# Sequence transform: right-hand sums as additions, and those of two products made by an adding DMA

## The chip, the cores and the metric

The kernel runs on one core of a Trainium2 chip. The metric is device time in microseconds (us), the median of several runs of the same program. A core has TensorE (PE, matrix products), VectorE (DVE), ScalarE (ACT), GpSimd (POOL) and SyncE (SP), each with its own queue of instructions that it works through in order; 16 DMA engines move blocks between HBM and the on-chip memory, and POOL, SP and ACT issue DMAs.

## The reference

The inputs are float32: x of 2048 x 1024, two 2048 x 2048 matrices of a sequence transform, two 1024 x 1024 matrices of a hidden transform, weights of a dense layer with 3584 hidden units, and a gate vector.

```python
g = sigmoid((x * gate_w).sum(-1, keepdims=True))
a = x @ Wd_re.T ;  b = x @ Wd_im.T              # hidden transform
y = Ws_re @ a - Ws_im @ b                       # sequence transform, real part
h = relu(x @ w1 + b1) ** 2 ;  o = h @ w2 + b2   # dense layer
return g * y + (1 - g) * o
```

## The kernel before, in words

There are four matrix stages, one after the other: X (the hidden transform, giving blocks `ab`), C (the sequence transform, giving `y`), H (first dense product) and O (second dense product). Between stages the blocks are kept in HBM tensors (`Kept`): `ab`, `h`, and `gy`, which is y times the gate.

Each stage cuts its product 2 x 2 and forms it from seven products instead of eight (Winograd's form), with sums S1 to S4 of left blocks and T1 to T4 of right blocks (L34 to L39). Within some products (`TWICE_C`) the same scheme is applied once more to part of the depth. Sign conventions: in C, the left blocks are `ab` and the right blocks are tiles of the input `ct`, the transposed transform matrices.

```python
TALL_C = (1, 2, 5, 6, 3, 7, 4)                    # order of the seven products (L19)
FACTORS = {... 5: ("S1", "T1"), 6: ("S2", "T2"), 7: ("S3", "T3")}
```

A block is 128 partitions x 1024 floats, 512 KB. Each operand block is split into a part `hi`, rounded by ScalarE (L221), and a rest `lo` = block - hi, made by VectorE (L231). A block product is then three matmuls per 128 x 128 tile: hi.hi, hi.lo, lo.hi (L307). Products 5, 6 and 7 of C go directly: 8 depth blocks x 2 column halves, 16 steps of 24 matmuls each. Per step there is one right sum, and per two steps one left sum.

A sum of two blocks that lie in HBM is a `Part` (L132). `load_parts` takes a buffer for each, and issues both loads on SP (L153). `make_parts` then has VectorE add or subtract them in place (L173), and frees the second buffer. T1 and T3 of product 5 and 7 are such sums of two `ct` blocks; T2 and T4 build on sums that are already on the chip, or on copies of them that POOL stores to HBM (`copy<-raw`) and SP fetches again.

The order of instructions is written out by a planner, the loop from L926. At step i of 434 it: issues loads up to 12 steps ahead (`LOADS`), as long as buffers are free and no more than `RAWS` = 4 blocks are loaded but not summed; issues the stores of results on POOL; makes sums and `hi` copies that are due within 3 steps (`SUMS`), or earlier if its own clock of VectorE says there is time; makes the `lo` rests due within 2 steps; then issues the step's matmuls. This fixes the order on each engine's queue. On the chip an engine goes ahead as far as its inputs and buffers allow, so SP, VectorE and ScalarE run some time ahead of TensorE.

When a product ends, its PSUM banks are copied to a buffer by ScalarE (`put`, L434), added to a buffer by VectorE (`add`, L440), or finished by `final` (L806 in C: y times the gate row, then a store to `gy` on POOL). The next product that builds on a buffer has ScalarE write it back into PSUM first (L294). The gate rows are fetched by `Row`; for O they are turned into 1 - g (L784).

Of the kernel before, what the change touches and what calls it, by code (L numbers as in the profile page):

```python
# [11 lines left out]
AF = mybir.ActivationFunctionType  # L12
# [30 lines left out]
def gated_mix_kernel(ctx: ExitStack, tc: tile.TileContext, x4, xn, w4, ct, w1a, w1b, w2, b1, b2, gw, out):  # L43
# [11 lines left out]
    nc = tc.nc  # L55
# [76 lines left out]
    class Part(Near):  # L132


        def __init__(self, a, b=None, op=None, width=512):
            super().__init__("part")
            self.blocks, self.op, self.width, self.copy = ([a] if b is None else [a, b]), op, width, None
            self.cuts = [(slice(0, 2), slice(0, width))]
            for e in self.blocks:
                if isinstance(e, (Near, View)):  # L140
                    e.uses += 1

        def room(self):
            return sum(not isinstance(b, (Near, View)) for b in self.blocks)

        def load_parts(self, engines):
            self.slots = [None if isinstance(b, (Near, View)) else take("raw") for b in self.blocks]
# [6 lines left out]
                yield  # L154

        def load(self, engines):
            run(self.load_parts(engines))

        def extra(self):
            return 0 if self.room() else 1  # L160

        def time(self):
            return VEC[0] + VEC[1] * self.width / 512 if self.op else 0.0

        def make_parts(self):
            for b in self.blocks:
                assert not isinstance(b, (Near, View)) or b.done
            src = [b.slot if isinstance(b, (Near, View)) else t for b, t in zip(self.blocks, self.slots)]
            mine = [t for t in self.slots if t is not None]
            self.slot, self.done = mine[0] if mine else take("sum"), True  # L170
            for k, c in self.cuts:
                if self.op:
                    nc.vector.tensor_tensor(self.slot[:, k, c], src[0][:, k, c], src[1][:, k, c], op=self.op)  # L173
# [153 lines left out]
            needs += group.done[count[group] // group.k - 1][1]  # L327
        wanted.append(needs)

    stores = []  # L330
    later, now = deque(), [0]
    clock = {"pe": 10.0, "vec": 0.0, "dma": 0.0}

# [3 lines left out]
    class Sums:  # L337


        def __init__(self, get, sums, keep=False, far=()):  # L340

            self.get, self.sums, self.keep, self.far, self.made = get, sums, keep, far, {}

        def of(self, key, width=512, near=False):
            if key in self.made:
                return self.made[key]
            if key not in self.sums:
                if not self.keep:
                    return self.get(*key)
                b = self.get(*key)  # L350
                e = b if isinstance(b, (Near, View)) else Part(b, width=width)
            else:
                a, b, op = self.sums[key]
                e = Part(*(self.of(p, width).far() if p in self.far and not near else self.of(p, width) for p in (a, b)), op, width)
            self.made[key] = e
            return e

# [52 lines left out]
                    ends[e] = len(steps)  # L410
        return ends

    def tall(left, right, ksteps, order, second, first, target, final, last=None):

# [1 line left out]

        left = {q: Sums(lambda i, j, q=q: left_(i, j, q), SUMS_L, far=FAR_TALL) for left_ in (left,) for q in range(ksteps)}
        right = {(q, c): Sums(lambda j, n, q=q, c=c: right_(j, n, q, c), SUMS_R, far=FAR_TALL) for right_ in (right,)
                 for q in range(ksteps) for c in range(2)}
        keys = [(c, rp) for c in range(2) for rp in range(2)]
# [12 lines left out]
        def add(dst, k, ps, ends=False, src=None, sign=1):  # L437
# [323 lines left out]
    class Row(Near):  # L761
# [1 line left out]

        ready = False

        def __init__(self, n, less):
            super().__init__("g")
            self.n, self.less, self.uses = n, less, 8

        def extra(self):  # L770
            return 0
# [7 lines left out]

        def sum(self):  # L780
            self.done = True
            if not self.less:
                return 0.0
            nc.vector.tensor_scalar(flat(self.slot), flat(self.slot), -1.0, 1.0, op0=ALU.mult, op1=ALU.add)  # L784
            return VEC[0] + VEC[1]

        def rest(self):
# [7 lines left out]
          for rp in range(2)}  # L795

    def c_stage():
        rows = [Row(n, False) for n in range(2)]
        to = {}

        def target(i, n, k):
            near = Near("y")
            to[near] = i, n, *k
            return near

        def final(dst, ps):  # L806
            i, n, c, rp = to[dst]
            nc.vector.tensor_tensor(dst.slot, dst.slot if ps is None else ps, rows[n].of(c).broadcast_to([P, 2, 512]),
                                    op=ALU.mult)
# [5 lines left out]
        tall(lambda i, j, q: ab[j, q, i], lambda j, n, q, c: ct[n, c, j, q], 8, TALL_C, TWICE_C, FIRST_C, target, final)  # L815
        return at, rows


    def o_stage():
        rows = [Row(n, True) for n in range(2)]  # L820
# [98 lines left out]
        o.landed = 0.0  # L919

    def ready(o):
        near = [o.block] if isinstance(o, Operand) else getattr(o, "blocks", ())
        return all(b.done for b in near if isinstance(b, (Near, View)))

    loaded = summed = rested = 4
    for i in range(-SUMS, n + LATER + 2):  # L926
# [5 lines left out]
        while loaded < len(items) and items[loaded].need <= i + LOADS:  # L932
# [11 lines left out]
            o.landed = clock["dma"] + LAND - RATE if o.room() else 0.0  # L944
            loaded += 1
        for dst, src, k, tiles in stores:
            if isinstance(dst, Kept):
# [73 lines left out]
```

## Time and profile before

| | us |
|---|---|
| three runs | 1882.75, 1888.65, 3587.61 |
| median | 1888.65 |
| span of the profiled execution | 1879.6 |
| TensorE matmul busy | 1866.2 |
| VectorE busy | 1686.0 |
| ScalarE busy | 1044.1 |
| GpSimd busy | 87.6 |

The span is the time from the first to the last instruction of one profiled execution; the time of a run also holds what lies around it, so the close runs lie 3.2 and 9.1 us above the span. The third run has almost twice the time of the others and is not used. A row of a group of instructions reads: line, engine, operation, what it writes and reads with shapes, count, busy time in all, mean ns of one, and the idle time just before them with what ended it. "L173" is line 173 of the kernel.

### The profile page before, as it was taken

The numbers are of one execution on the slowest core, as the hardware profiler recorded it, in microseconds if no ns is written. First come the engines' busy times: TensorE is split into PE (matmuls) and PEld (weight loads), VectorE is DVE, ScalarE is ACT, GpSimd is POOL, SyncE is SP. The second block draws the span as 40 slices with busy tenths as digits, with TensorE's granted clock in tenths as the row PEclk, the third lists the DMA queues.
The fourth block names the chain that finished last, engine by engine and source line by source line (L and its number), as shares of the span: only waits on it lengthen the run. The fifth ranks groups of instructions, "written<-read, shape, count | busy, mean of one in ns | idle before, by whom it ended". The sixth has DMA issues, their size and how long they took to land.

```text
span 1879.6 us, 22035 instructions
## 1 busy us (share of the span) xinstructions
PE 1866.2 (99%) x8228; PEld 1541.3 (82%) x8228; DVE 1686.0 (90%) x1638; ACT 1044.1 (56%) x1184; POOL 87.6 (5%) x162
## 2 busy tenths in 40 slices
PE   9999999999999999999999999999999999999998
PEld 7888888888888878888888888888888888887887
DVE  8997898599779898799996998799999998699898
ACT  6474563363343554366485797676977534264453
POOL 0000110000000000000000010000100000000000
PEclk9999999999999999999999999999999999999999
DMA  6732989439788379464461766536865798638971
GB/s 224 249 121 74 351 286 412 141 112 361 275 307 330 128 299 378 149 232 181 137 221 61 302 234 218 195 122 246 298 233 177 254 389 317 258 124 335 409 256 52
DMA packets 128570, 443.97 MB, mean 236 GB/s; under 512 B 14144, under 2 KB 23632, under 8 KB 128464
## 3 DMA queue, kind: packets, MB, share of 16 engines
q1 hardware_dynamic: 106560, 364.05, 53.7%
q0 software_dynamic: 21616, 78.14, 10.4%
q8 instruction: 64, 1.05, 0.2%
q10 hardware_dynamic: 288, 0.39, 0.1%
q14 instruction: 42, 0.34, 0.1%
HBM read 363.87 MB, written 78.65 MB: 235 GB/s over the span
## 4 chain that ended last, share of the span: by engine, by line
PE 94%; DVE 4%; DMA 1%; ACT 1%; issue 0%; SPq 0%; DVEq 0%; ACTq 0%
PE ps L307 94%; DVE lo L231 1%; DVE h L620 1%; DVE sum L173 1%; DMA raw<-in_x 0%; DVE u L503 0%; DMA raw<-in_w1b 0%; DMA g<-g_far 0%; DVE both L231 0%; DVE raw L173 0%; ACT ps L294 0%; ACT h L717 0%; ACT hi L221 0%; DVE o L505 0%; SPq L153 0%
## 5 line engine op out<-in xcount | busy, mean ns | idle before, releaser
L307 PE MATMUL ps<-hi 128*128 128x512 f32 x2168 | 844.3, 390 | 3.3 <-ACT hi L221 2.7
L307 PE MATMUL ps<-lo,hi 128*128 128x512 f32 x2168 | 844.1, 390 | 0.0
L307 PE MATMUL ps<-hi,lo 128*128 128x512 f32 x2168 | 843.3, 390 | 0.7 <-DVE lo L231 0.6
L221 ACT ACTIVATE hi<-raw 128x1024 fp32r<-128x1024 f32 (+2 forms) x398 | 406.8, 1037 | 370.6 <-DVE raw L173 245.7
L231 DVE TENSOR_TENSOR lo<-raw,hi 128x1024 fp32r<-128x1024 f32 (+2 forms) x398 | 468.3, 1197 | 45.5 <-ACT hi L221 28.4
L307 PEld LDWEIGHTS ps<-hi 128*128 128x128 f32 x2168 | 407.5, 188 | 89.7 <-ACT hi L221 3.5
L307 PEld LDWEIGHTS ps<-hi,lo 128*128 128x128 f32 x2168 | 407.6, 188 | 86.3 <-DVE lo L231 2.1
L307 PEld LDWEIGHTS ps<-lo,hi 128*128 128x128 f32 x2168 | 407.4, 188 | 84.4 <-DVE lo L231 0.4
L173 DVE TENSOR_TENSOR raw<-raw 128x1024 f32<-128x1024 f32 (+1 forms) x276 | 325.6, 1206 | 57.4 <-DMA raw<-in_ct 13.6
L307 PE MATMUL ps<-hi,both 128*128 128x512 f32 x1120 | 347.9, 390 | 3.1 <-ACT ps L294 3.1
L221 ACT ACTIVATE hi<-sum 128x1024 fp32r<-128x1024 f32 (+1 forms) x192 | 196.8, 1038 | 184.5 <-DVE sum L173 170.1
L231 DVE TENSOR_TENSOR lo<-sum,hi 128x1024 fp32r<-128x1024 f32 (+1 forms) x192 | 228.0, 1200 | 31.5 <-PE ps L307 18.2
L307 PEld LDWEIGHTS ps<-hi,both 128*128 128x128 f32 x1120 | 210.3, 188 | 49.4 <-ACT ps L294 5.5
L307 PE MATMUL ps<-lo,both 128*128 128x512 f32 x560 | 218.3, 390 | 0.1
L173 DVE TENSOR_TENSOR sum<-raw 128x1024 f32<-128x1024 f32 (+2 forms) x136 | 140.3, 1048 | 13.0 <-PE ps L307 9.3
L173 DVE TENSOR_TENSOR sum<-raw,sum 128x1024 f32<-128x1024 f32 (+2 forms) x102 | 112.4, 1107 | 13.3 <-PE ps L307 10.3
L307 PEld LDWEIGHTS ps<-lo,both 128*128 128x128 f32 x560 | 105.2, 188 | 22.0 <-DVE lo L231 0.6
L620 DVE TENSOR_TENSOR h<-h,ps 128x1024 f32<-128x1024 f32 x92 | 98.1, 1085 | 9.0 <-ACT u L613 7.0
L613 ACT ACTIVATE u<-ps 128x1024 f32<-128x1024 f32 x76 | 71.8, 952 | 51.6 <-PE ps L307 43.7
L294 ACT ACTIVATE ps<-u 128x1024 f32<-128x1024 f32 x79 | 76.9, 980 | 20.7 <-DVE o L848 7.1
L221 ACT ACTIVATE both<-sum 128x512 fp32r<-128x512 f32 x80 | 49.6, 625 | 58.6 <-DVE sum L173 43.6
L717 ACT ACTIVATE h<-h,b1c 128x512 f32<-128x512 f32 x112 | 74.3, 715 | 10.5 <-DVE h L620 10.2
(62 smaller groups left out, 724.2 us busy)
## 6 DMA issues: line engine op xcount, KB each, us to landing
raw<-in_ct SPq DMA_DIRECT2D x151, 512.0 KB, 6.9
raw<-h SPq DMA_DIRECT2D x134, 512.0 KB, 7.3
raw<-in_x SPq DMA_DIRECT2D x107, 512.0 KB, 4.9
raw<-in_w SPq DMA_DIRECT2D x98, 512.0 KB, 6.9
raw<-ab SPq DMA_DIRECT2D x72, 512.0 KB, 6.6
h<-h POOLq DMA_DIRECT2D x48, 512.0 KB, 5.9
raw<-in_w1a SPq DMA_DIRECT2D x36, 512.0 KB, 5.5
ab<-ab POOLq DMA_DIRECT2D x32, 512.0 KB, 6.4
```

Of the source, the lines that this page charges most:

```text
L173: nc.vector.tensor_tensor(self.slot[:, k, c], src[0][:, k, c], src[1][:, k, c], op=self.op)
L221: nc.scalar.activation(self.hi[:, k, c], self.block.slot[:, k, c], AF.Copy)
L231: nc.vector.tensor_tensor(self.lo[:, k, c], self.block.slot[:, k, c], self.hi[:, k, c].bitcast(F32), op=SUB)
L294: nc.scalar.activation(t[:, :n, :], b.slot[:, at:at + n, :], AF.Copy, scale=self.sign)
L307: nc.tensor.matmul(self.ps[r // self.per][:, r % self.per, :], a[:, kk, r * P:(r + 1) * P], b[:, kk, :], start=self.at == 1 and kk + n == ...
L613: nc.scalar.activation(view(near.slot, k), view(ps, k), AF.Copy, scale=float(sign))
L620: nc.vector.tensor_tensor(view(near.slot, k), view((src or dst)[k].slot, k), view(ps, k), op=ADD if sign > 0 else SUB)
L717: nc.scalar.activation(dst.slot[:, k, :], (dst.slot if ps is None else ps)[:, k, :], AF.Relu, bias=b1c[:, tile0 + k:tile0 + k + 1])
```

## The change

Only stage C changes its sums. The right sums there become additions only: T1 = (0,1) + (0,0), T2 = (1,1) + T1, T3 = (1,1) + (0,1), T4 = (1,0) + T2 where (j,n) names a right block. So that the products still give the transform, the left sums change signs too, and the second column half of the result comes out negated: its PSUM copies for product 5's target get the scale -1, and its gate row is multiplied by -1.

T1 and T3, the right factors of products 5 and 7, are then made while loading: SP loads the first block into one buffer, and POOL issues a DMA that adds the second block of HBM to the loaded buffer (`accum_op=ADD`). VectorE does nothing for them, and one buffer is taken instead of two. The add is put into POOL's queue two planner steps after the load (`ADD_LATER`), or when the operand is due within 3 steps. In the built order each of the 32 adds stands one step after its load.

In counts of the whole program: VectorE's block operations `raw<-raw` go from 260 to 220, and 8 scalar-tensor-tensor operations (S4, "minus both") and one scaling of a gate row are new; SP's loads of `ct` go from 151 to 119; POOL has 32 adding DMAs more. The matmuls and ScalarE's instructions keep their numbers, 8184 and the same kinds.

```diff
+ADD_LATER, LAND_SUM = 2, 20.0
+LANDING_C = "T1", "T3"
...
+SUMS_LT = {"S1": ((1, 0), (1, 1), SUB), "S2": ("S1", (0, 0), SUB), "S3": ((0, 0), (1, 0), SUB),
+           "S4": ("S2", (0, 1), "minus both")}
+SUMS_RT = {"T1": ((0, 1), (0, 0), ADD), "T2": ((1, 1), "T1", ADD), "T3": ((1, 1), (0, 1), ADD),
+           "T4": ((1, 0), "T2", ADD)}
...
         def room(self):
-            return sum(not isinstance(b, (Near, View)) for b in self.blocks)
+            return 1 if self.lands else sum(not isinstance(b, (Near, View)) for b in self.blocks)
+
+        def load_landing(self, engines):
+            self.slot, self.added = take("raw"), False
+            a, b = (b.at if isinstance(b, Kept) else b for b in self.blocks)
+            next(engines).dma_start(self.slot, a)
+            landing.append((now[0] + ADD_LATER, self, b))
+
+        def add_landing(self, b):
+            nc.gpsimd.dma_start(self.slot, b, accum_op=ADD)
+            self.added = True
...
         def make_parts(self):
+            if self.lands:
+                assert self.added
+                self.done = True
+                yield
...
+                if self.op == "minus both":
+                    nc.vector.scalar_tensor_tensor(self.slot[:, k, c], src[0][:, k, c], -1.0, src[1][:, k, c],
+                                                   op0=ALU.mult, op1=SUB)
...
-                nc.scalar.activation(flat(near.slot), flat(ps), AF.Copy)
+                nc.scalar.activation(flat(near.slot), flat(ps), AF.Copy, scale=float(minus) if dst is c22 else 1.0)
...
-        rows = [Row(n, False) for n in range(2)]
+        rows = [Row(n, (-1.0 if n and LANDING_C else 1.0, 0.0)) for n in range(2)]
...
+        while landing and (landing[0][0] <= i or landing[0][1].need <= i + SUMS):
+            _, o, b = landing.popleft()
+            o.add_landing(b)
```

More of the change, by code (lines that the diff above doesn't have):

```diff
@@ L137, in __init__ @@
             self.blocks, self.op, self.width, self.copy = ([a] if b is None else [a, b]), op, width, None
+            self.lands, self.added = False, None
             self.cuts = [(slice(0, 2), slice(0, width))]
@@ L156, in load @@
         def load(self, engines):
-            run(self.load_parts(engines))
+            if self.lands:
+                self.load_landing(engines)
+            else:
+                run(self.load_parts(engines))
         def extra(self):
@@ L162, in time @@
         def time(self):
-            return VEC[0] + VEC[1] * self.width / 512 if self.op else 0.0
+            return VEC[0] + VEC[1] * self.width / 512 if self.op and not self.lands else 0.0
         def make_parts(self):
+            if self.lands:
+                assert self.added
+                self.done = True
+                yield
+                if self.copy:
+                    stores.append((self.copy, self, 0, 2))
+                return
             for b in self.blocks:
@@ L328, in step @@
         wanted.append(needs)
-    stores = []
+    stores, landing = [], deque()
     later, now = deque(), [0]
@@ L337, in gated_mix_kernel, with __init__ @@
     class Sums:
-        def __init__(self, get, sums, keep=False, far=()):
+        def __init__(self, get, sums, keep=False, far=(), landing=()):
             self.get, self.sums, self.keep, self.far, self.made = get, sums, keep, far, {}
+            self.landing = landing
         def of(self, key, width=512, near=False):
@@ L354, in of @@
                 e = Part(*(self.of(p, width).far() if p in self.far and not near else self.of(p, width) for p in (a, b)), op, width)
+                e.lands = key in self.landing
             self.made[key] = e
@@ L411, in seven, with tall @@
         return ends
-    def tall(left, right, ksteps, order, second, first, target, final, last=None):
-        left = {q: Sums(lambda i, j, q=q: left_(i, j, q), SUMS_L, far=FAR_TALL) for left_ in (left,) for q in range(ksteps)}
-        right = {(q, c): Sums(lambda j, n, q=q, c=c: right_(j, n, q, c), SUMS_R, far=FAR_TALL) for right_ in (right,)
+    def tall(left, right, ksteps, order, second, first, target, final, last=None, landing=()):
+        sums_l, sums_r = (SUMS_LT, SUMS_RT) if landing else (SUMS_L, SUMS_R)
+        left = {q: Sums(lambda i, j, q=q: left_(i, j, q), sums_l, far=FAR_TALL) for left_ in (left,) for q in range(ksteps)}
+        right = {(q, c): Sums(lambda j, n, q=q, c=c: right_(j, n, q, c), sums_r, far=FAR_TALL, landing=landing) for right_ in (right,)
                  for q in range(ksteps) for c in range(2)}
+        minus = -1 if landing else 1
         keys = [(c, rp) for c in range(2) for rp in range(2)]
@@ L764, in gated_mix_kernel, with __init__ @@
         ready = False
-        def __init__(self, n, less):
+        def __init__(self, n, scale):
             super().__init__("g")
-            self.n, self.less, self.uses = n, less, 8
+            self.n, self.scale, self.uses = n, scale, 8
         def extra(self):
@@ L781, in sum @@
             self.done = True
-            if not self.less:
+            if self.scale == (1.0, 0.0):
                 return 0.0
-            nc.vector.tensor_scalar(flat(self.slot), flat(self.slot), -1.0, 1.0, op0=ALU.mult, op1=ALU.add)
+            nc.vector.tensor_scalar(flat(self.slot), flat(self.slot), *self.scale, op0=ALU.mult, op1=ALU.add)
             return VEC[0] + VEC[1]
@@ L814, in c_stage @@
         at = len(steps)
-        tall(lambda i, j, q: ab[j, q, i], lambda j, n, q, c: ct[n, c, j, q], 8, TALL_C, TWICE_C, FIRST_C, target, final)
+        tall(lambda i, j, q: ab[j, q, i], lambda j, n, q, c: ct[n, c, j, q], 8, TALL_C, TWICE_C, FIRST_C, target, final,
+             landing=LANDING_C)
         return at, rows
     def o_stage():
-        rows = [Row(n, True) for n in range(2)]
+        rows = [Row(n, (-1.0, 1.0)) for n in range(2)]
         to = {}
@@ L921, in ready @@
     def ready(o):
+        if getattr(o, "lands", False) and not o.added:
+            return False
         near = [o.block] if isinstance(o, Operand) else getattr(o, "blocks", ())
@@ L943, in gated_mix_kernel @@
             clock["dma"] = max(clock["dma"], start) + RATE * o.room()
-            o.landed = clock["dma"] + LAND - RATE if o.room() else 0.0
+            o.landed = clock["dma"] + (LAND_SUM if getattr(o, "lands", False) else LAND) - RATE if o.room() else 0.0
             loaded += 1
```

2 lines of the change are left out of this document (1 added, 1 removed).

## The prediction

> **What bounds the kernel now.** I read the page's busy shares first, then its chain of work that ended last, then busy time by stage.
>
> ```profile
> span 1879.6 us, 22035 instructions
> ...
> PE 1866.2 (99%) x8228; PEld 1541.3 (82%) x8228; DVE 1686.0 (90%) x1638; ACT 1044.1 (56%) x1184; POOL 87.6 (5%) x162
> ...
> PE 94%; DVE 4%; DMA 1%; ACT 1%; issue 0%; SPq 0%; DVEq 0%; ACTq 0%
> ```
>
> TensorE is busy for 1866.2 of 1879.6 us and carries 94% of the chain. A busy PE need not be PE at its peak, so the second look is at its rate. In the view of busy time by stretches, a row gives the stretch, its length, then busy time and count of each engine, the granted clock, the DMA share and GB/s:
>
> ```profile
> 100.00:200.00 100.00, 100.00 (x443) 82.87 (x442) 88.78 (x78) 57.92 (x61) 2.13 (x4) 1.00 0.33 117
> ...
> 450.00:880.00 430.00, 428.67 (x1887) 353.68 (x1886) 378.79 (x361) 194.62 (x210) 15.99 (x30) 1.00 0.70 262
> ```
>
> In an undisturbed stretch 443 matmuls pass in 100 us at clock 1.00: 0.2257 us each, so a step of 24 matmuls takes 5.42 us and a product of 16 steps 86.7 us. The change adds and removes no matmul. In the sequence stage (450 to 880 us) PE stands idle for 430.00 - 428.67 = 1.3 us. **That is all a better-fed PE can win in the stage**; over the whole kernel, beginning included, it is 1879.6 - 1866.2 = 13.4 us, 0.7%. VectorE's 90% is not what ends last.
>
> The profiled execution has a span of 1879.6 us; the two close runs of before, 1882.75 and 1888.65 (the median), lie 3.2 and 9.1 us above it, 6.1 on average. I sum against the span and add 6.1.
>
> **The change part by part.** These are groups of instructions, each with count, busy time, mean ns, and idle time before it:
>
> ```profile
> L173 DVE TENSOR_TENSOR raw<-raw 128x1024 f32<-128x1024 f32 x260 | 311.1, 1222 | 52.7 <-DMA raw<-in_ct 13.6 <-DMA raw<-in_w 10.9 <-DMA raw<-in_x 9.5
> ...
> L748 DVE SCALAR_TENSOR_TENSOR raw<-raw,gwb 128x1024 f32<-128x1024 f32 x16 | 19.0, 1221 | 0.0
> ...
> L784 DVE TENSOR_SCALAR g<-g 128x1024 f32<-128x1024 f32 x2 | 1.4, 692 | 0.4 <-DMA g<-g_far 0.4
> ```
>
> *VectorE.* T1 and T3 are needed for 8 depths and 2 column halves each: 32 sums of 1.222 us leave VectorE, 39.1 us in all (16 in product 5, 16 in product 7). Eight sums S4 turn from a subtraction into a scalar-tensor-tensor operation: 1.222 to 1.221 us by the gate's row, nothing. One more scaling of a gate row is 0.69 us. VectorE should fall from 1686.0 to 1647.6 us. Since PE waited 1.3 us in the stage, I credit **0**. The evictions with scale -1 keep their instruction; I cost them 0.
>
> *SP and POOL.* 32 plain loads of 512 KB leave SP's queue, and 32 fewer buffers are taken, and 32 adding DMAs enter POOL's. In the built order each add stands one step behind its load and about three ahead of its use. Ahead of PE the engines run by buffers, so the timeline tells the real lead:
>
> ```profile
> 428.13 0.81 SPq L153 DMA_DIRECT2D raw<-ab  x2
> ...
> 496.32 10.83 SPq L153 DMA_DIRECT2D raw<-in_ct  x4
> ...
> 440.41 3.49 DVE L173 TENSOR_TENSOR raw<-raw 128x1024 f32<-128x1024 f32 x3
> ...
> 441.73 3.28 ACT L221 ACTIVATE hi<-raw 128x1024 fp32r<-128x1024 f32 x3 [3.45 <-DVE raw L173]
> ...
> 448.74 0.53 POOL L128 DMA_DIRECT2D gy<-y  x1 [20.26 <-DVE y L808]
> ...
> 452.42 0.39 PE L307 MATMUL ps<-hi 128*128 128x512 f32 x1
> ...
> 676.10 0.80 SPq L153 DMA_DIRECT2D raw<-ab  x2
> ...
> 794.90 0.39 PE L307 MATMUL ps<-hi,both 128*128 128x512 f32 x1
> ```
>
> Product 5 starts on PE at 452.42 (the first matmul without a "both" operand), its first left blocks are asked for at 428.13 (the first right blocks just before), and its last right block among those of 496.32. Product 7 ends at 794.90, where product 4's "both" operands begin; its first left blocks are asked for at 676.10. The sums of product 5 began at 440.41, 12 us before PE wanted them.
>
> **The new wait.** ScalarE's copy `hi` (L221) of T1 or T3 now waits for the add's landing where it waited for VectorE (the 3.45 us above). Behind it on ScalarE stand the other `hi` copies and, at the seams of products, the PSUM refills at L294, for which PE waits. Each add waits on POOL for its own load; behind it stand later adds and the `gy` stores. The first seven adds of product 5 and the first eight of product 7 are placed ahead of the `gy` stores that wait for the end of the product before (the row at 448.74); the operands of the others are wanted from the eighth step on, 452.42 + 7 x 5.42 = 490, so that queue costs nothing. At the start: landing of a load,
>
> ```profile
> DMA to landing us min/median/max: 3.1/6.9/15.8
> ...
> L221 ACT ACTIVATE hi<-raw 128x1024 fp32r<-128x1024 f32 x369 | 385.7, 1057 | 356.0 <-DVE raw L173 241.3 <-PE ps L307 48.5 <-DMA raw<-in_ct 25.5
> ...
> L231 DVE TENSOR_TENSOR lo<-raw,hi 128x1024 fp32r<-128x1024 f32 x369 | 443.3, 1221 | 35.7 <-ACT hi L221 23.9 <-PE ps L307 9.0 <-DMA copy<-raw 1.1
> ```
>
> (the first line is that of the blocks of in_ct, issue to landing) even an add that takes the worst 15.8 us from about 430 lands at 446; hi 1.06 and lo 1.22 end at 448.3, before 452.42. Latency is covered; if that cover were gone, each product would start one landing late, 2 x 6.9 = 14 us.
>
> **What the adding DMA costs the engines** is the open term; no row of before has one. The stage's DMA load:
>
> ```profile
> 430.00:480.00 50.00, 50.00 (x222) 41.46 (x221) 49.95 (x48) 19.34 (x19) 1.60 (x3) 1.00 1.02 409
> 480.00:530.00 50.00, 50.00 (x223) 41.43 (x222) 34.56 (x30) 13.69 (x13) 1.60 (x3) 1.00 0.70 241
> 530.00:590.00 60.00, 60.00 (x266) 49.72 (x265) 49.81 (x45) 26.27 (x26) 6.39 (x12) 1.00 0.97 368
> ...
> 600.00:610.00 10.00, 10.00 (x46) 8.29 (x45) 9.27 (x11) 4.65 (x6) 0.00 (x0) 1.00 0.50 174
> ...
> 670.00:760.00 90.00, 89.86 (x396) 73.82 (x394) 84.40 (x78) 40.44 (x41) 2.15 (x4) 1.00 0.97 370
> 760.00:790.00 30.00, 30.00 (x134) 24.86 (x133) 18.25 (x22) 8.38 (x12) 0.00 (x0) 1.00 0.18 65
> ```
>
> The engines are full when a product's blocks come (share 1.02 at 409 GB/s): a 524 KB block takes 524/409 = 1.28 us of all 16, though it lands 6.9 us after its issue, so transfers overlap. Now p is the engines' time of one add. Per product there are 16 plain right blocks, 16 left blocks and 16 adds, less the first right pair, loaded earlier: 30 x 1.28 + 16p = 38.4 + 16p us. The room of product 5 runs from 428.13 to the start of its last step, 452.42 + 15 x 5.42 = 533.7, less hi, lo and one landing (2.3 + 6.9), less four `gy` stores (5.1): 91 us. That of product 7 runs from 676.10 to 794.90 - 5.42 = 789.5, less the same: 99 us. What does not fit stalls PE:
>
> stall = max(0, 16p - 53) + max(0, 16p - 61).
>
> Bounds: at least 1.28 (as a plain block; below that nothing, since a block is still moved), at most 15.8 (the worst landing, with nothing beside it). An add reads the block and its target and writes once; in a full queue, where rows show transfers overlapping, I take it as two plain blocks, **p = 2.56**. Then 16p = 41: both terms are 0, with 12 and 20 us to spare. What is late next is product 6: 16 x 1.28 = 20.5 us more DMA work meets 0.30 x 50 = 15 us of idle engines between 480 and 530, so its blocks come some 5 us later, and share falls to 0.50 by 600 while PE stays on product 6 until 452.42 + 2 x 86.7 = 626. Nothing reaches PE. After product 7 the share is 0.18.
>
> The Trainium skill's page Collectives: The Full Stack, section "The bandwidth ceiling: the fold count and why AG ≠ RS ≠ AR", says that an add in the DMA engines halves the rate because it reads two sources; by it p would be 2.56 and the stall 0. No run here shows that yet.
>
> Sum: 1879.6 + 0 + 6.1 = 1885.7, say **1886 us**.
>
> **The rivals.**
>
> *Adds that do not overlap (slower).* An add must read its target before it writes; if the engines finish one before they take the next, p is two lone landings, 2 x 3.1 = 6.2 us. Then 16p = 99: stalls of 46 and 38, 84 us together, and 1879.6 + 6.1 + 84 = 1970 us. For it: the engines are full exactly there (1.02), and nothing here shows an overlap of adds. Against it: plain transfers overlap five deep (6.9 over 1.28). It starts to cost at p = 3.3. It is slower by 2% than the median at 1.02 x 1888.65 = 1926, 41 us over the sum: 32p - 114 = 41, p = 4.84. At the far end, p = 15.8, it is 200 + 192 = 392 us, 2278 us.
>
> The skill's page DMA: Bandwidth & Descriptors, section "Two DMAs through the same engine are not ordered", tells of read-modify-write packets of which the second still read stale data when it closely followed the first; by it neighbouring adds overlap and this rival is weakened. No run here shows it.
>
> *VectorE's relief pays (a little faster).* If waits elsewhere in the stage go with the 39.1 us, PE gains at most its 1.3 us there: 1884 us. Even all of the kernel's 13.4 us would give 1872, under 1%. Over 2% is out of PE's reach.
>
> *The work is moved, not saved.* The wait of `hi` goes from VectorE to the adds and each product starts a landing late: 1886 + 14 = 1900 us. The 12 us of lead speak against it.
>
> **How the numbers follow.** The forecast has 0.40, the small gain 0.05, the late starts 0.08: together 0.53 within 2%, which is about what a measurement of this kernel can tell from no change. Adds that do not overlap have 0.45: the term is unmeasured, its bounds span a factor of 12, and everything above 4.84 is slower. Of this, 0.32 lies up to p = 7.5, where the stall is 32 x 7.5 - 114 = 126 us and the time 2012; 0.13 above it is left out. Faster by 2% has 0.02. The range runs from PE's floor, 1872, to 2012; the within-2% cases alone span 1872 to 1905.
>
> **What would show it.** In the profile after: 32 POOL DMAs raw<-in_ct; VectorE at 1648 us; ScalarE's hi waiting for DMA where it waited for L173. Right: PE still full from 450 to 880 with 443 per 100 us, and a DMA share near 1 from 430 into the 520s. Wrong: PE idle in products 5 and 7 behind ACT hi, the adds' landing times growing from one to the next, the DMA share at 1 with fewer GB/s than 409. The prediction fails if an add costs the engines over 4.84 us, or if its making on POOL takes longer than the 5.42 us of a step.

## The result and the profile after

The changed kernel takes 1915.21 us (median, 1911.64 to 1920.21); the kernel before, on the same chip, 1885.70 us. One of the four runs of before, at 3587.61 us, counts in that median (1882.75 us without it) and is left out of the ratio, which is **1.0169, 95% interval 1.0141 to 1.0198**: 1.7% slower, inside the 2% that counts as no change here, but the interval excludes 1. The forecast was 1886.

The page of the changed kernel: span, busy time by engine, the chain that ended last, the two main DMA queues, and two groups (busy time, mean ns, idle time before them and what ended it).

```profile
span 1918.4 us, 22007 instructions
...
PE 1877.1 (98%) x8228; PEld 1545.1 (81%) x8228; DVE 1648.9 (86%) x1607; ACT 1040.9 (54%) x1184; POOL 115.2 (6%) x194
...
q1 hardware_dynamic: 101952, 347.27, 50.0%
q0 software_dynamic: 26224, 94.92, 14.8%
...
PE 79%; DVE 9%; DMA 7%; issue 3%; ACT 2%; SPq 0%; POOL 0%; DVEq 0%; POOLq 0%; ACTq 0%
...
L337 PE MATMUL ps<-hi 128*128 128x512 f32 x2168 | 846.4, 391 | 26.5 <-ACT ps L324 21.8
...
L251 ACT ACTIVATE hi<-raw 128x1024 fp32r<-128x1024 f32 (+2 forms) x398 | 404.5, 1036 | 421.7 <-DVE raw L203 188.9
```

VectorE fell to 1648.9 us, as worked out (1647.6). TensorE has the same 8228 matmuls (the 8184 counted with the change and 44 others), but its idle time rose from 13.4 to 1918.4 - 1877.1 = 41.3 us, and its busy time by 10.9. Together that is 38.8 us, the whole difference of the two spans (the two profiled executions lie further apart than the medians, 29.5 us: the profiled one of after is the longest of its four).

Where: the view of busy time by stretches (length, then busy time and count of PE, PEld, DVE, ACT and POOL, granted clock, DMA share, GB/s), first of the changed kernel, then of the kernel before.

```profile
420.00:520.00 100.00, 99.94 (x442) 82.34 (x441) 60.01 (x56) 31.43 (x33) 14.38 (x19) 1.00 0.94 279
...
440.00:480.00 40.00, 39.95 (x177) 32.75 (x176) 25.18 (x23) 13.75 (x14) 6.80 (x9) 1.00 1.05 316
480.00:520.00 40.00, 40.00 (x179) 33.10 (x178) 15.78 (x14) 10.16 (x10) 5.09 (x6) 1.00 0.93 273
...
540.00:560.00 20.00, 10.29 (x39) 8.09 (x38) 11.53 (x10) 8.61 (x9) 1.61 (x3) 0.74 0.88 308
...
700.00:750.00 50.00, 36.45 (x143) 28.59 (x144) 30.37 (x28) 17.13 (x17) 9.94 (x13) 0.87 1.04 318
```

```profile
440.00:480.00 40.00, 40.00 (x178) 33.17 (x177) 39.95 (x36) 17.01 (x16) 1.60 (x3) 1.00 1.03 412
480.00:520.00 40.00, 40.00 (x179) 33.13 (x178) 27.30 (x24) 12.32 (x12) 0.53 (x1) 1.00 0.68 234
```

Product 5, the first with adds, runs at full rate (442 matmuls in 100 us against 443 before). In this stage TensorE starves in two places above all, both at **seams** between products: at 540 to 560, where product 6 follows 5, and at 700 to 750, where product 7 follows 3. At the undisturbed rate 0.2257 us per matmul the first stretch lacks 88.6 - 39 = 49.6 matmuls, 11.2 us, and the second 221.5 - 143 = 78.5, 17.7 us: 28.9 us, most of the loss. Of the other 10 us of this execution, some 5 lie far behind, in stage O: from 1720 to 1740 us 58 matmuls pass, where the row of before that holds this place (1680 to 1700) has 81. The profiles of e4_plain and e18_signstraffic below lose about as much there, those of e2_t1 and e3_t3 don't; this was not followed, and the rest is spread thinly.

What TensorE waits for from 420 to 900 us, in the view of waits (us in all, times, longest), changed kernel, then before:

```profile
PE ps L337 <- ACT ps L324: 22.8, 5, 9.7
PE ps L337 <- DVE lo L261: 2.0, 3, 1.3
PE ps L337 <- ACT hi L251: 0.9, 1, 0.9
```

```profile
PE ps L307 <- ACT ps L294: 1.2, 2, 0.6
```

`ACT ps` is the refill: ScalarE copies a half-finished block back into PSUM, and the next product's first matmuls add onto it. ScalarE is not short of time (54% busy); the refill stands **behind `hi` copies in ScalarE's queue**. Its timeline at the second seam, before (start, us, instruction, idle time before it and what ended it):

```profile
697.82 3.33 ACT L221 ACTIVATE hi<-raw 128x1024 fp32r<-128x1024 f32 x3 [3.48 <-DVE raw L173]
701.23 1.03 ACT L294 ACTIVATE ps<-u 128x1024 f32<-128x1024 f32 x1
704.63 1.03 ACT L294 ACTIVATE ps<-u 128x1024 f32<-128x1024 f32 x1 [2.37 <-DVE y L808]
706.89 1.03 ACT L294 ACTIVATE ps<-u 128x1024 f32<-128x1024 f32 x1 [1.24 <-DVE y L808]
```

and after:

```profile
706.23 1.06 ACT L251 ACTIVATE hi<-raw 128x1024 fp32r<-128x1024 f32 x1 [8.18 <-DMA raw<-in_ct]
709.93 2.00 ACT L251 ACTIVATE hi<-raw 128x1024 fp32r<-128x1024 f32 x2 [2.64 <-DMA raw<-in_ct]
...
726.84 1.06 ACT L251 ACTIVATE hi<-raw 128x1024 fp32r<-128x1024 f32 x1 [6.88 <-DMA raw<-in_ct]
730.59 2.00 ACT L251 ACTIVATE hi<-raw 128x1024 fp32r<-128x1024 f32 x2 [2.69 <-DMA raw<-in_ct]
732.50 1.01 ACT L324 ACTIVATE ps<-u 128x1024 f32<-128x1024 f32 x1
735.59 1.06 ACT L251 ACTIVATE hi<-raw 128x1024 fp32r<-128x1024 f32 x1 [2.08 <-DMA raw<-in_ct]
736.55 1.96 ACT L324 ACTIVATE ps<-u 128x1024 f32<-128x1024 f32 x2
```

Before, three refills follow each other from 701.23 and wait at most for VectorE's last evictions. After, the first refill comes at 732.50, when the last `hi` copy ahead of it has its add. VectorE is held as well: its second eviction of product 3 comes at 733.76, behind a `lo` that waited 6.94 us for `hi`. The built order moved too: between the last refill of product 3 (`ps<-y`) and the four of product 7 (`ps<-u`), ScalarE's queue had a last unbroken run of 8 `hi` copies, three refills, one copy, one refill; now it has 12 copies, a refill, one copy, two refills, two copies, a refill. At the first seam the order is the same in both kernels. The chain at that seam, in order of time (start, us, what):

```profile
540.47 7.04 DMA raw<-in_ct
...
547.60 1.24 DVE raw L203
...
548.86 1.06 ACT hi L251
549.92 0.91 ACT y L468
...
551.77 0.93 ACT ps L324
```

Here it is a plain load of product 6, landing at 547.51, that a sum, a `hi` copy and through them the refill wait for; product 6 was due at 539 by the forecast's own times. The load was not slow (7.04 us) but late: it belongs to a burst of 10 that SP issues from 540.05 on, and from 528.83 before. SP's timeline (start, us, instruction), before and after:

```profile
528.83 17.30 SPq L153 DMA_DIRECT2D raw<-in_ct  x10
```

```profile
540.05 19.73 SPq L170 DMA_DIRECT2D raw<-in_ct  x10
```

### The profile page after: what moved, and what is told of

The parts are those of the page before. It is cut to its first block, busy times and chain, and to the rows that moved or that the text cites. A ratio compares the mean times of both kernels' runs of the same rounds, so it can differ in the third digit from the quotient of the medians.

```text
span 1918.4 us, 22007 instructions
## 1 busy us (share of the span) xinstructions
PE 1877.1 (98%) x8228; PEld 1545.1 (81%) x8228; DVE 1648.9 (86%) x1607; ACT 1040.9 (54%) x1184; POOL 115.2 (6%) x194
## 3 DMA queue, kind: packets, MB, share of 16 engines
q0 software_dynamic: 26224, 94.92, 14.8%
q8 instruction: 64, 1.05, 0.2%
## 4 chain that ended last, share of the span: by engine, by line
PE 79%; DVE 9%; DMA 7%; issue 3%; ACT 2%; SPq 0%; POOL 0%; DVEq 0%; POOLq 0%; ACTq 0%
PE ps L337 79%; DMA raw<-in_ct 4%; DVE lo L261 3%; DVE sum L203 2%; DMA raw<-ab 1%; DMA gy<-y 1%; DVE h L654 1%; ACT hi L251 1%; DVE raw L203 1%; ACT ps L324 0%; DVE u L537 0%; DVE both L261 0%; DMA raw<-in_x 0%; DVE y L474 0%; DMA raw<-in_w1a 0%
## 5 line engine op out<-in xcount | busy, mean ns | idle before, releaser
L203 DVE TENSOR_TENSOR raw<-raw 128x1024 f32<-128x1024 f32 (+1 forms) x236 | 277.2, 1199 | 62.3 <-DMA raw<-h 14.1
L203 DVE TENSOR_TENSOR sum<-raw,sum 128x1024 f32<-128x1024 f32 (+2 forms) x102 | 111.9, 1102 | 10.6 <-PE ps L337 10.1
```

## The experiments

Three theories stood against each other: **landing** (the second landing comes too late for ScalarE's copies, and so for the refills behind them), **engine time** (an add costs the 16 DMA engines more than a plain load, and all loads behind it come later) and **the POOL queue** (stores of finished blocks stand behind adds and hold their buffers). Ratios are to the kernel before, on the same chip.

### The signs alone, and one product at a time

```diff
 # e1_signs: both blocks loaded and summed on VectorE, signs as in the change
-                e.lands = key in self.landing
+                e.lands = False
 # e2_t1: adds in product 5 only; e3_t3: in product 7 only
-LANDING_C = "T1", "T3"
+LANDING_C = ("T1",)      # e3_t3: ("T3",)
```

> The turned signs alone: all right sums are additions made by VectorE, no adding DMA. If the cost sits in the adding DMAs, the time is that of before, 1880 to 1890 us, with PE full from 530 to 560 us and from 690 to 750 us. If it sits in the turned signs (scaled evictions, S4, the gate row), it stays near 1915.

> Only T1 (product 5) is made by adding DMAs; T3 (product 7) is summed by VectorE. By the profile after, PE lost 10 us and some clock at the seam from product 5 to 6, and 14 us and some clock at the seam from 3 to 7. So this should give before plus 10 to 13 us, about 1896 us, with the idle PE at 540 to 560 alone. If the two seams are linked (the first pushes the second late), it gives nearer to 1885 or 1915.

> Only T3 (product 7) is made by adding DMAs. By the same rows: before plus 15 to 19 us, about 1902 us, with the idle PE at 700 to 740 alone. Together with the run with T1 alone the two gains should add up to the 29 us of the change if the seams are independent.

Measured: e1_signs 1884.18 us, ratio 0.9999 [0.9986, 1.0012]; e2_t1 1896.40, 1.0061 [1.0041, 1.0081]; e3_t3 1901.65, 1.0097 [1.0074, 1.0119]. The signs, the scalar-tensor-tensor operations and the second gate row cost nothing. Each set of adds makes the one seam that it touches late (e2_t1 at 540 to 560, e3_t3 at 700 to 740), and the two losses nearly add up: 0.61 + 0.97 = 1.58% of the 1.69%.

### The second DMA as a plain copy

The second block overwrites the first: the landing stays, the engine time of the add goes.

```diff
 # e4_plain
-            nc.gpsimd.dma_start(self.slot, b, accum_op=ADD)
+            nc.gpsimd.dma_start(self.slot, b)
 # e10_longer: a third landing, of 64 bytes per partition, ahead of it
+            nc.gpsimd.dma_start(self.slot[:, 0, :16], b[:, 0, :16])
+            nc.gpsimd.dma_start(self.slot, b)
```

> The second DMA on POOL copies its block over the first instead of adding it (the sum is left out: the products use the second block alone). The chain load, then a second transfer, then the hi copy is kept; the price of the adding in the engines goes (2.8 to about 1.3 us of the 16 engines). If the chain of two landings ahead of ScalarE's copies is the cause, most of the 29 us stays: 1900 to 1912 us. If the engine time of the adding is the cause, the time goes back to 1883 to 1890 us.

> A plain copy takes the place of the add, and ahead of it POOL copies 64 bytes per partition into the same buffer, so that the chain has three landings and takes some 3 to 5 us longer at hardly any engine time (the sums T1 and T3 are left out: products 5 and 7 use the second block alone). Plain copies without the small one gave 1895. If the add costs by the time until it lands, this gives 1905 to 1918 us; if it costs by the engines' time, it stays at 1894 to 1899 us.

Measured: e4_plain 1895.14 us, 1.0056 [1.0033, 1.0078], between what the two theories gave; e10_longer 1905.92, 1.0109 [1.0082, 1.0135]. Issue to landing on POOL's queue, median us, in the changed kernel and then in e4_plain:

```profile
raw<-in_ct POOLq DMA_DIRECT2D x32, 512.0 KB, 10.1
```

```profile
raw<-in_ct POOLq DMA_DIRECT2D x32, 512.0 KB, 7.1
```

A second landing by itself costs a third of the loss, and a third landing as much again. In stage C the second landing costs at one seam only. Stretches of e4_plain:

```profile
540.00:560.00 20.00, 20.00 (x90) 16.56 (x89) 18.37 (x16) 10.09 (x11) 2.12 (x4) 1.00 0.88 304
700.00:720.00 20.00, 15.86 (x59) 12.55 (x58) 18.47 (x17) 10.12 (x11) 4.79 (x9) 0.83 0.99 387
```

The seam at 540 is whole again; the one at 700, where the order on ScalarE has changed, still stalls. SP's burst of 10 loads is back at its old time as well:

```profile
529.04 16.78 SPq L170 DMA_DIRECT2D raw<-in_ct  x10
```

So a plain second landing explains part of the second seam and nothing of the first. A longer one could do more: an add lands 3 us later than this copy, and e10_longer, with its third landing, is late at a new place, the start of product 5 (402 matmuls from 420 to 520 us in place of 443). Its burst comes at 539.39 us, and its seam at 540 is whole (90 matmuls) with product 5 itself some 9 us behind.

### Adds that nobody waits for, and buffers

Two tries gave the adds to spare buffers that nobody reads; products 5 and 7 then use the first block alone. In e9_spare a one-column copy on POOL keeps each add at its place; e5_nowait differs in that its column goes to a place of its own.

```diff
 # e9_spare
+    spare = deque(take("spare") for _ in range(2))
...
-            nc.gpsimd.dma_start(self.slot, b, accum_op=ADD)
+            spare.append(spare.popleft())
+            nc.gpsimd.tensor_copy(spare[-1][:, 0, :1], self.slot[:, 0, :1])
+            nc.gpsimd.dma_start(spare[-1], b, accum_op=ADD)
 # e11_fewer: signs only, two buffers fewer
-SLOTS, KEEP, RAWS = 55, 5, 4
+SLOTS, KEEP, RAWS = 53, 5, 4
```

> The 32 adding DMAs keep their place on POOL, their wait for the load and their source in HBM, but add into two spare buffers that nobody reads (the sums T1 and T3 are left out: products 5 and 7 use the first block alone; two buffers fewer for the rest). The engines do the same work; no copy of ScalarE waits for an add. If the wait for the landing of the add is the cause, the time goes back to 1883 to 1892 us. If the engine time of the adds delays the other blocks, it stays at 1900 to 1915 us.

> The run without waiters again, with the adds held in their place: POOL first copies one column of the loaded block into the spare buffer, so each add follows its load; it adds into one of two spare buffers that no engine reads (T1 and T3 are left out: products 5 and 7 use the first block). Engine work as in the changed kernel, no ScalarE copy waits for an add. Wait theory: 1883 to 1893 us. Engine theory, in which the adds take the engines from the other blocks: 1900 to 1912 us. Two buffers are missing; what that alone costs is measured beside it.

> The turned signs alone, with 53 buffers instead of 55: the control of the run with two spare buffers. If buffers are not short, 1884 us as with 55; if they are, 1890 us or more, to be taken off the run with spare buffers.

Measured: e5_nowait 1946.44 us, 1.0328 [1.0307, 1.0349]; e9_spare 1941.37, 1.0288 [1.0263, 1.0314]; e11_fewer 1902.27, 1.0084 [1.0058, 1.011]. The first two settle nothing: in e5_nowait the adds had moved to the first 130 us of the kernel; in e9_spare POOL stood waiting for the spare buffers and the stores behind it. Both gave up two buffers, and e11_fewer shows that this alone costs 16 us. A wait of e9_spare's TensorE, 420 to 900 us:

```profile
PE ps L343 <- ACT ps L330: 34.5, 4, 26.3
```

One wait of 26.3 us came from a blocked POOL queue, which made that queue the suspect for what follows.

### Earlier loads, later copies

The order was loosened around the adds: up to 10 buffers of loads ahead where there were 4 (e6_deep), the `hi` copies of T1 and T3 one step later (e7_later), both (e8_both), and both with the plain second copy (e12_bothplain).

```diff
 # e6_deep
-            if o.need > i + SUMS and o.room() + sum(e.room() for e in items[summed:loaded]) > RAWS:
+            limit = 10 if any(getattr(e, "lands", False) for e in items[summed:loaded + 1]) else RAWS
+            if o.need > i + SUMS and o.room() + sum(e.room() for e in items[summed:loaded]) > limit:
 # e7_later
-            if o.need > i + (RESTS if lo else SUMS):
+            lands = getattr(o, "lands", False) or getattr(getattr(o, "block", None), "lands", False)
+            if o.need > i + (RESTS if lo else SUMS - lands):
```

> Around T1 and T3 up to 10 blocks instead of 4 may be loaded ahead of their sums: the loads and adds stand 8 to 10 steps ahead of their use in the built order instead of 4. The adds cost the engines the same. If the wait for the add's landing is the cause, most of the 29 us goes: 1883 to 1895 us. If engine time is the cause, nothing much changes, 1905 to 1915. If buffers are the limit, it stays or gets worse, since blocks hold their buffers longer.

> The hi copies of T1 and T3 stand one step later in ScalarE's order (2 steps ahead of use instead of 3); by the planner's own rule their loads then come one step later too, 3 steps ahead of use. If the trouble is that the copies stand ahead of the refills of PSUM at the seams, the stall at product 7 shrinks: 1900 to 1910 us. If it is the short way from load to use, it grows: 1918 to 1935 us.

> Both edits: loads and adds 6 to 10 steps ahead, hi copies 2 ahead. Wait theory: at least as good as the deep loads alone, 1882 to 1892 us, since the copies find their blocks landed and stand behind the refills. Engine theory: 1905 to 1915 us.

> Deep loads and later hi copies, and a plain copy in the place of the add (the sums T1 and T3 are left out: products 5 and 7 use the second block). With adds this gave 1900.7. If what was left there is the engines' time for adding, it goes: 1883 to 1888 us. If what was left is the chain or the order, 1895 to 1900 us.

Measured: e6_deep 1910.84 us, 1.0138 [1.0117, 1.0158]; e7_later 1917.14, 1.0183 [1.0149, 1.0216]; e8_both 1900.69, 1.0086 [1.0065, 1.0106]; e12_bothplain 1889.98, 1.0021 [1.0006, 1.0035]. Only both together help clearly, and they win back half, which lies between what the theories gave for e8_both. With them the plain copy costs 4 us and the add 16 (by the ratios): between an add and a plain second copy 12 us remain that this loosening of the order does not take away.

### The stores off the POOL queue

In the changed kernel SP once waited 23.2 us for the landing of a `gy` store, which stood behind adds. The view of SP's waits from 476 to 500 us:

```profile
SPq L156 <- DMA gy<-y: 23.2, 1, 23.2
```

```diff
 # e13_gyact (e16_gysp: nc.sync); e14_signsgy: the same with e.lands = False; e15_bothgy: on e8_both
+            self.name = name
...
-            nc.gpsimd.dma_start(self.at[:, k:k + tiles, :], src[:, :tiles, :])
+            (nc.scalar if self.name.startswith("gy") else nc.gpsimd).dma_start(self.at[:, k:k + tiles, :], src[:, :tiles, :])
```

> The changed kernel with its 32 stores of output blocks in stage C (gy) issued on ScalarE's queue and not on POOL's; the 32 adds are the same. In the changed kernel a gy store issued 7 to 11 us later than before and landed 14.3 us after its issue, and SP once waited 23.2 us for such a landing. Theory of the POOL queue (stores behind adds hold the buffers): SP's 23.2 us wait goes, the stall at 540 to 560 us shrinks to under 3 us, 1885 to 1900 us, ratio 1.000 to 1.008. Theory of the second landing (ScalarE's copies wait for the adds): both stalls stay, 1908 to 1918 us. Theory of engine time: the same 1908 to 1918 us.

> Control: signs turned, no adding DMA, and the gy stores on ScalarE's queue. What the move of the stores costs by itself: all theories expect 1880 to 1892 us; what it lies above 1884 is to be taken off the result of e13_gyact.

> Deeper loads and later copies around the adds (e8_both, 1900.7 us) and the gy stores on ScalarE's queue. Theory of the POOL queue: what was left goes as well, 1883 to 1892 us. Theory of the second landing: 1898 to 1903 us, since the stores had nothing to do with it. Theory of engine time: 1898 to 1903 us.

> As e13_gyact, with the gy stores on SP's queue, among the loads: they leave the adds' queue as well, but SP can be held up by them, since it is the queue that issues the loads. Theory of the POOL queue: 1885 to 1905 us. Theories of the second landing and of engine time: 1908 to 1925 us.

Measured (the trace has 16 such stores, not the 32 of the expectation): e13_gyact 1912.69 us, 1.0148 [1.0127, 1.017]; e14_signsgy 1886.49, 1.0003 [0.9988, 1.0017]; e15_bothgy 1900.12, 1.0079 [1.0053, 1.0105]; e16_gysp 1909.51, 1.0136 [1.0113, 1.016]. The move itself is free, and by the ratios it wins 4 and 6 us of the 32 (1.69%); the intervals overlap that of the changed kernel. TensorE's waits in e13_gyact are as in the changed kernel:

```profile
PE ps L338 <- ACT ps L325: 21.3, 4, 10.1
```

The POOL queue is not the main cause. SP's long wait was no proof of it either: e13_gyact still has one of 19.6 us for a `gy` store, now off POOL's queue, and e4_plain one of 15.6 us, with its seam at 540 whole. In e16_gysp SP's longest wait for a `gy` store is 5.6 us, and its burst of 10 loads still comes at 535.93.

### The engine time without adds

The last two kernels give the engines extra transfers in the place of the adds' extra time: each `hi` block of T1 and T3 is also stored to a place in HBM that nobody reads, from ScalarE's queue. e17_plaintraffic does it on e4_plain, e18_signstraffic on e1_signs, where there is no second landing.

```diff
 # e17_plaintraffic and e18_signstraffic, behind the copy that makes hi
+            if getattr(self.block, "traffic", False):
+                nc.scalar.dma_start(dram.tile([P, 2, 512], F32, name=f"idle{len(idles)}"), self.hi.bitcast(F32))
+                idles.append(self)
```

> As e4_plain (the second block overwrites the first by a plain DMA, the 32 sums are left out of the output; 1895.1 us), and each of the 32 blocks' leading part (hi) is also stored once to a place in HBM that nobody reads, on ScalarE's queue right behind the copy that makes it: 32 times 512 KB of transfer, some 1.3 us of all 16 engines each, which is nearly what an add takes more than a plain DMA (2.76 less 1.31). Nobody waits for these stores and they hold no buffer that is wanted soon. Theory of engine time: the stretches at the seams are full (DMA share 1.0 and more), so the loads behind come later, 1906 to 1916 us, as the changed kernel. Theory of the landing: 1893 to 1899 us, as e4_plain.

> As e1_signs (signs turned, no adding DMA; 1884.2 us) with the same 32 stores that nobody waits for. No second landing at all, only the engine time. Theory of engine time: 1893 to 1906 us, some 10 to 20 us over e1_signs. Theory of the landing: 1882 to 1889 us.

Measured: e17_plaintraffic 1915.99 us, **1.0168 [1.0147, 1.0188]**; e18_signstraffic 1898.92, **1.0082 [1.0065, 1.0099]**. (There is no profile of e17_plaintraffic at this time, so its stretches aren't read.) The changed kernel's 1.0169 is met without one add. What the stores cost the engines is read from the queues: first POOL's queue before (21616 packets, 78.14 MB), then ScalarE's in e18_signstraffic, and ScalarE's before.

```profile
q0 software_dynamic: 21616, 78.14, 10.4%
...
q10 hardware_dynamic: 288, 0.39, 0.1%
```

```profile
q10 hardware_dynamic: 4896, 17.17, 2.2%
```

POOL's queue before: 10.4% of 1879.6 = 195.5 us of all 16 engines for 149 blocks of 0.524 MB, 1.31 each. After: 14.8% of 1918.4 = 283.9, that is 88.4 more for 32 adds, **2.76 each**. An add costs 1.45 more than a plain block. Against a plain copy in its own place, in e4_plain, it is much the same:

```profile
q0 software_dynamic: 26224, 94.92, 12.7%
```

12.7% of 1894.0 = 240.5, that is 45.0 more than before for 32 copies, 1.41 each, and an add costs 1.35 more. The stores of e18_signstraffic take (2.2% of 1897.7 - 0.1% of 1879.6)/32 = 1.24 each, a little less than that. And they make the first seam late. Stretches of e18_signstraffic:

```profile
540.00:560.00 20.00, 14.28 (x52) 11.25 (x51) 14.91 (x13) 10.41 (x11) 1.07 (x2) 0.83 0.98 363
...
700.00:760.00 60.00, 60.00 (x266) 49.71 (x265) 48.88 (x43) 23.07 (x22) 2.15 (x4) 1.00 1.02 407
```

SP's burst of 10 loads comes late here too, with no add in the kernel:

```profile
537.69 15.71 SPq L170 DMA_DIRECT2D raw<-in_ct  x10
```

So the loss has two parts, and the four kernels show them. With neither second landing nor extra stores: 0.9999. Second landing alone: 1.0056, in stage C seen at the seam of product 7 (88.6 - 59 = 29.6 matmuls, 6.7 us). Extra stores alone: 1.0082, with the seam at 540 lacking 88.6 - 52 = 36.6 matmuls (8.3 us, over half of the loss) and product 7's start whole. Both: 1.0168, and the add 1.0169. The parts sum to 1.38%; the other 0.3% is about as large as the intervals.

The extra stores are not engine time alone, though. SP's waits of e18_signstraffic from 420 to 560 us have a row for their landings:

```profile
SPq L170 <- DMA idle<-hi: 13.5, 4, 4.5
```

So these stores also held up loads by their own landings. That engine time makes the first seam late is therefore the best reading, not a proof: it fits e18_signstraffic, which has no second landing, and e4_plain, which has hardly any extra engine time. How much of it is the wait for the stores in e18_signstraffic, and in the changed kernel the longer landing of an add (10.1 against 7.1 us), stays open.

What stays open besides: at the seam of product 7, how much is the second landing and how much the changed order on ScalarE (12 copies ahead of the first refill in place of 8). No run kept the old order with two landings. Nor was a kernel run with its refills put ahead of the copies. No version was found that beats the kernel before; the best with all 32 adds is e15_bothgy at 1.0079.

## Why the prediction was wrong

**What bounds the kernel.** Right. VectorE lost 37.1 us of busy time and nothing was gained; the 0 credited to it stands, and e1_signs has the small edits at 0 as well.

**The price of an add.** Right: 2.56 forecast, 2.76 measured. The rival "adds that do not overlap" at p = 6.2 and 1970 us is refuted: an add lands 10.1 us after its issue and takes 2.76 of the engines, and POOL issues two of them 1.26 us apart (at 452.16 and 453.42), so several are under way together. The Trainium skill's page Collectives: The Full Stack, section "The bandwidth ceiling: the fold count and why AG ≠ RS ≠ AR", which halves the rate for an add, agrees with the trace: 2.76 / 1.31 = 2.1.

**The ledger of the engines' room.** This is the first step that failed, and not by its price: with 2.76, 16p = 44, its two terms (53 and 61) still give 0. Within product 5 it held, 442 matmuls in 100 us. What failed is the step behind it: "its blocks come some 5 us later, and share falls to 0.50 by 600 while PE stays on product 6 until 452.42 + 2 x 86.7 = 626. Nothing reaches PE." Product 6's first blocks are due when it starts, at 452.42 + 86.7 = 539, not when it ends. The engines that were idle for a third of 480 to 520 (share 0.68) are now busy (0.93), and the burst of product 6's loads moves back by 11.2 us, from 528.83 to 540.05; TensorE waits up to 9.7 us for a refill behind them, and the seam loses 11.2 us where the forecast had 0. That each late load holds up the next through the buffers is argued, not shown. e18_signstraffic shows such a late seam with no add in the kernel, with the doubt named above.

**The new wait.** This is the second step that failed. The text named the place, "the PSUM refills at L294, for which PE waits", behind `hi` on ScalarE, and then priced it at nothing because product 5's first sums lay 12 us ahead. That lead was read at one place and used for two. At the start of product 7 the rows show less: the last `hi` copies ahead of the first refill ended at 701.15, the refill ran from 701.23 to 702.26, and product 7 was due 6 us later by the forecast's own times (794.90 - 86.7 = 708.2). A landing more (a median of 7.1 us for the plain copies of e4_plain, 10.1 for the adds) does not fit in there. The seam lost 17.7 us; e4_plain shows 6.7 of them lost with a plain second landing and no extra engine time. The step also missed that the copies would move ahead of the refills.

**The POOL queue, "that queue costs nothing".** Nearly right: 4 to 6 us by e13_gyact and e16_gysp, at the edge of what they can tell. It looked at adds behind stores only, while the stores now stand behind adds.

**The rivals and the range.** "The work is moved, not saved" (1900 us, one landing late per product) was the nearest in mechanism and in time, and it had 0.08: it had the landing, but not the engines. The time lies within the range of 1872 to 2012, but 10 us above the 1905 that the cases within 2% were given. Of the signs of being wrong, one came true as written: a DMA share of 1.05 at 316 GB/s where it was 1.03 at 412. The idle time was foreseen in products 5 and 7 behind `hi`; it came at the starts of 6 and 7, behind refills that stood behind `hi`. Neither condition named for failing was met, an add over 4.84 us of the engines (2.76) or over 5.42 us of POOL (0.86).

## What to carry to other kernels

A ledger of engine time has to be closed at each point where work falls due, above all at the start of the next product, and not only at the end of the one that is changed: transfers that fit into an idle stretch take it from the prefetch of what follows. Where an engine's queue mixes copies that wait for data with the refills that the bounding engine needs, list what stands ahead of each refill, in the built order, and its lead at every seam. An adding DMA frees VectorE at the price of about a plain DMA more and a second landing. Here VectorE did not bound, and nothing came back for that price; whether it pays where VectorE bounds and the DMA engines have time, no run here shows.

## What had not been expected of the hardware

- **An idle TensorE comes back slow.** In the row of 540 to 560 us after, the granted clock is 0.74 and 39 matmuls take 10.29 us, 0.264 us each in place of 0.2257. The timeline of PE in the changed kernel shows the first matmul after the longest wait, and two of those behind it:

```profile
552.74 0.79 PE L337 MATMUL ps<-hi 128*128 128x512 f32 x1 [9.71 <-ACT ps L324]
...
553.76 0.63 PE L337 MATMUL ps<-hi,lo 128*128 128x512 f32 x1
554.19 0.63 PE L337 MATMUL ps<-hi 128*128 128x512 f32 x1
```

  They start 0.43 us apart, nearly twice 0.2257, until about 556 us; from there on matmuls take 0.39 again. So the waits cost more than their length: of the 38.8 us between the spans, 27.9 are idle time and 10.9 longer busy time for the same 8228 matmuls. The Trainium skill's page TensorE: Matmul & The Clock Gate, section "Part 1: The HAM clock gate (the "warmup" mystery)", says that the clock halves after an idle window of about 3.4 us; the starts 0.43 us apart behind 9.71 us of idle time agree. In 1720 to 1740 us the granted clock is 0.83, though no wait there is longer than 1.8 us: there a few short waits did the same.
- **A lower granted clock with no lower rate.** The profiled execution of e3_t3 shows 0.95 in an undisturbed stretch, and yet 443 matmuls in 100 us:

```profile
100.00:200.00 100.00, 100.00 (x443) 82.83 (x442) 88.76 (x78) 57.92 (x60) 2.13 (x4) 0.95 0.33 118
```

- **Buffers are worth more than the sums.** Two of 55 buffers less cost 0.84% [0.58, 1.1] (e11_fewer), as much as the extra stores of e18_signstraffic.
- **An adding DMA holds POOL longer as well**: the group of the adds, against that of the copies' stores on the same queue, in the changed kernel.

```profile
L160 POOL DMA_DIRECT2D raw<-in_ct x32 | 27.4, 860 | 311.7 <-DMA raw<-in_ct 156.0 <-DVE y L474 96.8 <-PE ps L337 23.8
...
L134 POOL DMA_DIRECT2D copy<-raw x30 | 16.1, 536 | 188.6 <-DVE raw L203 188.6
```
